# Shifted hidden columns: writing them contiguously from a strided PSUM read, four loads per small weight, and a new order table

## The chip, the cores and the metric

The kernel runs on one core of one Trainium2 chip. The metric is the device time of one execution in microseconds (us); the number given for a kernel is the median of several executions. A profiled execution is one more run, and its span (first to last instruction) is a little shorter than its device time.

## The reference

One sequence of S = 2048 rows with D = 512 columns passes through four residual layers, A, B, A, B, each with a layer norm ahead of it. A is attention with 32 heads of 16 columns over 8 positions at distances 0, 2, ..., 14. B is a mixer:

```
h  = gelu(layernorm(x) @ w1)                      # 2048 x 512
g0 = h[:,   0:128] shifted by +1 row              # rows outside are zero
g1 = h[:, 128:256] shifted by -1 row
g2 = h[:, 256:384] shifted by +2 rows
g3 = h[:, 384:512] shifted by -2 rows
x1 = x + concat(g0, g1, g2, g3) @ w2
out = x1 + gelu(layernorm(x1) @ w3) @ w4          # w3: 512 x 1792, w4: 1792 x 512
```

The change sits in the shift of the four column groups of h.

## The kernel before

**Units of work.** The 2048 rows are four blocks of 512, and there are two passes over them (layers A and B, then A and B again), so the work comes as eight blocks n = 0 to 7. A block has four row tiles of 128 rows. Row tiles are interleaved: tile i of a block holds the row pairs 2i, 2i+1, then the pair eight rows further on, and so on (`rows`). For a block the phases are `p1_stream` (q, k, v through TensorE), `p2_unit` (attention, nearly all on VectorE, four units to a block), `p3` (output projection with wo, a layer norm, the product with w1, gelu, and the shifted h), `p4` (product with w2, the second layer norm) and `p5` (w3, gelu, w4, for fourteen slices of 128 hidden columns).

**Precision.** All products from block 1 on are done in float16 with each operand split into a high and a low half (three matmuls for a product, `HLS`). So h is stored twice: half 0 is gelu(...) scaled and rounded to float16, half 1 is the remainder. In block 0 the `p5` products are plain float32 (`plain_chunk`).

**How h is made.** In `p3`, for each group g of 128 hidden columns, twelve matmuls fill one PSUM buffer of kind "mm" with h transposed: 128 hidden columns on the partitions, 512 rows of the block along the free axis. ScalarE applies gelu in place, then copies the PSUM tile to half 0 of h (`to(0)` from `of()`), and VectorE writes half 1 with one `scalar_tensor_tensor` (`to(1)`). For g = 0 and 1 the shift is by one row, which crosses from a row tile to its neighbour, so the destination `to` walks h in float16 with steps of 127 elements between neighbours, while PSUM is read in order. For g = 2 and 3 the shift by two rows moves whole pairs, and both sides are contiguous. Rows that cross the wrapped end of a tile are then put in their place by copies within h: `move` to the cells "L" (g = 0, 2) and "R" (g = 1, 3), of 126 or 252 elements for each partition, and to "Le" and "Re" (one or two columns for each half, from or to the block next door). GpSimd (POOL) or VectorE does them. A tile of h has HW = 640 columns for each half and group; `p4` reads the 128 columns for row tile i at `RD[g] + P * i`.

**Order.** Nothing is scheduled at run time. Every piece of work is an operation with one or more alternatives (the same work on ScalarE, VectorE or POOL). The table `ORDER` lists all 3135 operations; an entry k stands for operation k // 4 done by its alternative k % 4. Each engine, and the SyncE queue (SP) that issues the DMAs, works through its own part of that list strictly in order. The table `SLOTS` says which physical buffer each logical buffer gets: there are four PSUM buffers "mm" and four "acc", five "f32" row tiles, two of "h", and so on. An operation that writes a buffer waits until all users of what was in it are done. So a PSUM buffer with a group of h in it is free only after gelu, half 0 and half 1.

**Small weights.** `small_weight` loads wo, w1 or w2 (512 x 512 float32, 1 MB) with one DMA into a buffer of kind "nT" or "h", takes its sum of squares (`square`), a matmul with ones (`power_of`), and splits it into halves. The buffer "h" that w1 goes into holds a part of wqkv at first, and is free when the first block's q, k, v products are done.

Every instruction is recorded by one helper, so all lines in the profile read L281.

Of the kernel before, what the change touches and what calls it, by code (L numbers as in the profile page):

```python
# [8 lines left out]
F32 = mybir.dt.float32  # L9
BF16 = mybir.dt.bfloat16  # L10
I32 = mybir.dt.int32
AF = mybir.ActivationFunctionType
# [5 lines left out]
P = 128  # L18
S = 2048
D = 512  # L20
# [12 lines left out]
HW = 640  # L33
# [234 lines left out]
def tile_mixer(ctx, tc, x_d, wqkv_d, wo_d, w1_d, w2_d, w3_d, w4_d, out_d):  # L268
# [575 lines left out]
    def p2_unit(n, qt):  # L844
# [76 lines left out]
        else:  # L921
            turn_split(ko, o, oT, [0], lambda: hl(0), lambda: hl(1), [o], scale=c_o)
        return oT

    RD = (0, P, 0, P)
    hs, n1_st, mixed = {}, {}, {}

    def late(h, g, first, pairs):
# [308 lines left out]
```

## Time and profile before

| | |
|---|---|
| median of 3 runs | 1246.36 us (1244.55 to 1248.82) |
| profiled execution | 1247.58 us |
| its span | 1245.8 us |
| mean granted TensorE clock | 0.977 |
| TensorE (PE) busy | 1166.2 us, 94%, 5324 matmul instructions |
| VectorE (DVE) busy | 955.5 us, 77% |
| ScalarE (ACT) busy | 586.0 us, 47% |
| GpSimd (POOL) busy | 441.7 us, 35% |

In the rows of the profile, an entry such as `h<-mm,c_h` names what is written and what is read; `mm` is a PSUM buffer, `w_hl` the halves of w1 or w2, `nT` a transposed normalized block. `[3.24 <-DVE h]` behind a TensorE row says that TensorE sat idle for 3.24 us ahead of it and what the wait ended with. A matmul's listed time is its latency; the distance between the starts of two groups of twelve is what they cost.

### The profile page before, as it was taken

Reading aid. Unit: us, or ns where it says so; the run is one execution under the profiler, and the core shown is the slowest. Engines: PE = TensorE matmul, PEld = TensorE weight load, DVE = VectorE, ACT = ScalarE, POOL = GpSimd, SP = SyncE. Lnnn points to the kernel's source line nnn. Section 1 sums busy time; section 2 is a strip of 40 time slices with the busy share of each in tenths; the row PEclk is TensorE's granted clock in tenths of the full one; section 3 lists DMA queues with packets and bytes.
Section 4 is the critical chain, followed back from the end, with each engine's and each line's share of the span. In section 5 each row is a group of like instructions: output and inputs, shape, how many; then the busy total and the mean of one; then the engine's idle time right before and its main releaser. Section 6 shows DMA issues by size and latency. Waiting matters only on the chain. (4 is left out here: it accounts for less than half of the span.)

```text
span 1245.8 us, 15079 instructions
## 1 busy us (share of the span) xinstructions
PE 1166.2 (94%) x5324; PEld 551.6 (44%) x5324; DVE 955.5 (77%) x990; ACT 586.0 (47%) x984; POOL 441.7 (35%) x502
## 2 busy tenths in 40 slices
PE   9769999899698999999999998999899999889997
PEld 7434444454243444444444443444344344434553
DVE  6889899998888899549998998699858997223311
ACT  5465454333856645435362356354455454433421
POOL 3110443204556354422672445344254141313000
PEclk9979999899999999999999998999999999999999
DMA  6765683464789546665479563976369366304321
GB/s 222 255 193 145 189 270 104 127 196 154 211 209 304 159 114 159 158 200 188 127 189 259 186 179 81 243 217 168 81 174 261 110 136 186 93 28 117 102 92 53
DMA packets 240388, 206.79 MB, mean 166 GB/s; under 512 B 107132, under 2 KB 167796, under 8 KB 240312
## 3 DMA queue, kind: packets, MB, share of 16 engines
q1 hardware_dynamic: 238088, 204.04, 57.4%
q10 hardware_dynamic: 2224, 1.79, 0.4%
q8 instruction: 42, 0.69, 0.2%
q14 instruction: 34, 0.28, 0.1%
HBM read 141.03 MB, written 39.47 MB: 145 GB/s over the span
## 5 line engine op out<-in xcount | busy, mean ns | idle before, releaser
L281 PE MATMUL mm<-nT,w 128*128 128x512 f16 (+1 forms) x1288 | 306.8, 392 | 9.3 <-DMA w<-w 4.2
L281 PE MATMUL acc<-w,g 128*128 128x512 f16 (+1 forms) x1260 | 306.6, 394 | 0.0
L281 PE MATMUL mm<-wq_hl,xt 128*128 128x512 f16 x1008 | 229.4, 384 | 8.5 <-DMA xt<-g 3.8
L281 ACT ACTIVATE mm<-mm,s_w 128x512 f32<-128x512 f32 (+1 forms) x144 | 92.5, 643 | 225.4 <-PE mm L281 225.2
L281 POOL TENSOR_TENSOR g<-f,g 128x512 f16<-128x512 f32 x80 | 126.7, 1589 | 197.4 <-ACT g L281 98.1
L281 PEld LDWEIGHTS <-w 128*128 128x128 f16 x1344 | 125.3, 98 | 151.2 <-issue 7.8
L281 PEld LDWEIGHTS <-g 128*128 128x128 f16 x1176 | 114.6, 98 | 137.0
L281 PEld LDWEIGHTS <-xt 128*128 128x128 f16 x1008 | 99.3, 99 | 130.2 <-issue 12.2
L281 DVE TENSOR_TENSOR prod<-kv,L 128x4096 f32<-128x4096 f32 x32 | 141.2, 4413 | 0.2
L281 DVE TENSOR_REDUCE L<-prod 128x256 f32<-128x4096 f32 x32 | 141.1, 4410 | 0.1
L281 DVE TENSOR_TENSOR prod<-kv,q 128x4096 f32<-128x4096 f32 x29 | 129.8, 4475 | 9.3 <-DMA kv<-kvq_d 8.8
L281 DVE TENSOR_TENSOR prod<-prod 128x2048 f32<-128x2048 f32 x64 | 117.0, 1829 | 0.2
L281 DVE SCALAR_TENSOR_TENSOR g<-mm,c_g,g 128x512 f16<-128x512 f32 x56 | 41.8, 747 | 97.0 <-ACT g L281 94.1
L281 PE MATMUL mm<-nT,w_hl 128*128 128x512 f16 x384 | 93.5, 397 | 18.5 <-DVE h L281 10.8
L281 PE MATMUL mm<-w_hl,h 128*128 128x512 f16 x384 | 90.9, 393 | 9.1 <-DVE h L281 8.2
L281 PE MATMUL mm<-wo_hl,oT 128*128 128x512 f16 x384 | 86.3, 380 | 0.0
L281 POOL TENSOR_SCALAR b<-b 128x1 f32<-128x1 f32 (+1 forms) x48 | 28.4, 591 | 155.4 <-ACT junk L281 153.4
L281 POOL COPY h<-h 128x126 f16<-128x126 f16 (+3 forms) x40 | 37.2, 949 | 128.0 <-DVE h L281 102.2
L281 DVE SCALAR_TENSOR_TENSOR h<-mm,c_h,h 128x512 f16<-128x512 f32 x32 | 51.0, 1625 | 36.8 <-ACT h L281 36.5
L281 PEld LDWEIGHTS <-w_hl 128*128 128x128 f16 x384 | 38.7, 101 | 70.5 <-issue 29.1
L281 ACT ACTIVATE g<-mm,c_g 128x512 f16<-128x512 f32 x98 | 66.7, 685 | 2.4 <-ACT mm L281 0.4
L281 PEld LDWEIGHTS <-h 128*128 128x128 f16 x384 | 38.5, 101 | 58.4 <-issue 16.9
(183 smaller groups left out, 1361.8 us busy)
## 6 DMA issues: line engine op xcount, KB each, us to landing
w<-w SPq DMA_DIRECT2D x196, 256.0 KB, 2.9
kv<-kvq_d SPq DMA_DIRECT2D x62, 768.0 KB, 5.8
kvq_d<-ev SPq DMA_DIRECT2D x84, 256.0 KB, 3.0
w<-in_B_w_dram SPq DMA_DIRECT2D x56, 256.0 KB, 3.5
w<-g SPq DMA_DIRECT2D x28, 256.0 KB, 4.0
q<-kvq_d SPq DMA_DIRECT2D x28, 256.0 KB, 3.6
w<-in_A_x_dram SPq DMA_DIRECT2D x16, 256.0 KB, 4.2
x<-in_A_x_dram SPq DMA_DIRECT2D x16, 256.0 KB, 4.3
```

Of the source, the lines that this page charges most:

```text
L281: i = f(*a, **k).ins
```

## The change

1. `HW` falls from 640 to 576. The h tile is no longer the rows in one run with spare columns at an end, but three runs: for g = 0 and 2 the first three shifted tiles in columns 0 to 383 and the wrapped one at 384; for g = 1 and 3 the wrapped one at `TAIL` = 388. `COL` replaces `RD`.
2. Both halves are written contiguously. The shift of g = 0 and 1 is now in the pattern by which PSUM is read (steps of two elements and of 127). Each copy becomes two instructions, one of 384 and one of 128 elements for each partition, for all four groups, on ScalarE (`early`) and on VectorE (`later`).
3. The wrapped tile lands in place, so the copies to "L" and "R" are gone (32 operations). The edge copies "Le" and "Re" and the clears stay, and are contiguous.
4. `small_weight` issues four DMAs of 256 KB, one for each 128 rows, where there was one of 1 MB. That is nine DMAs more.
5. "f32" has six buffers instead of five.
6. `ORDER` and `SLOTS` are new tables, for 3112 operations. Of the 518 TensorE operations, 437 stand at another place in TensorE's own sequence. The alternatives differ too: VectorE has 836 operations instead of 871, ScalarE 817 before and 836 now, POOL 285 before and 269 now.

```diff
-HW = 640
+HW = 576
+TAIL = 388
...
-        "f32": places("f32", 5, [P, D], F32),
+        "f32": places("f32", 6, [P, D], F32),
...
-        dma(key - 3.0, lambda: v().rearrange("p (c f) -> p c f", c=NC),
-            lambda: wd.rearrange("(c p) f -> p c f", p=P), [], [(st, c) for c in range(NC)], begun)
+        for c in range(NC):
+            dma(key - 3.0, lambda c=c: v()[:, D * c:D * c + D], lambda c=c: wd[P * c:P * c + P], [], [(st, c)], begun)
...
-    RD = (0, P, 0, P)
+    COL = ((3 * P, 0, P, 2 * P), (0, P, 2 * P, TAIL))
...
-            def to(a, g=g):
+            def parts_of(a, g=g, ps=ps):
+
                 v = blocks(h.t, HW)[:, a, g]
+                e = 2 if g > 1 else 1
+                c0 = 3 * P + e if g % 2 == 0 else TAIL - e
+                t0, s0 = (3 * P, 0) if g % 2 == 0 else (0, P)
                 if g < 2:
-                    return at(v[:, 1:], [list(v.ap[0]), [P, NT], [2, 64], [P - 1, 2]])
-                return v[:, P:] if g == 2 else v[:, :D]
-
-            def of(ps=ps, g=g):
-                return ps.t.rearrange("p (i k r) -> p i k r", i=NT, r=2) if g < 2 else ps.t
+                    src = [at(ps.t[:, 1:], [list(ps.t.ap[0]), [P, 3], [2, 64], [P - 1, 2]]),
+                           at(ps.t, [list(ps.t.ap[0]), [2, 64], [3 * P + 1, 2]])]
+                else:
+                    src = [ps.t[:, s0:s0 + 3 * P], ps.t[:, t0:t0 + P]]
+                return zip((v[:, :3 * P], v[:, c0:c0 + P]), src)
+
+            def early(parts_of=parts_of):
+                for o, i_ in parts_of(0):
+                    A.activation(o, i_, AF.Copy, scale=c_h.t)
+
+            def later(parts_of=parts_of):
+                for (o, i_), (hi, _) in zip(parts_of(1), parts_of(0)):
+                    V.scalar_tensor_tensor(o, i_, c_h.t, hi, ALU.mult, ALU.subtract)
...
-            act(key, lambda of=of, to=to: A.activation(to(0), of(), AF.Copy, scale=c_h.t),
-                [ps, c_h], [(h, (g, 0))])
-            dve(key, lambda of=of, to=to: V.scalar_tensor_tensor(
-                to(1), of(), c_h.t, to(0), ALU.mult, ALU.subtract), [ps, (h, (g, 0)), c_h], [(h, (g, 1))])
+            act(key, early, [ps, c_h], [(h, (g, 0))])
+            dve(key, later, [ps, (h, (g, 0)), c_h], [(h, (g, 1))])
...
-                move((h, ("L", g)), lambda g=g, n_=n_: late(h, g, 2, n_), lambda g=g, n_=n_: late(h, g, D, n_), own)
...
-                move((h, ("R", g)), lambda g=g, n_=n_, f0=f0: late(h, g, D + f0, n_),
-                     lambda g=g, n_=n_, f0=f0: late(h, g, 2 + f0, n_), own)
...
-                    c0 = RD[g] + P * i
+                    c0 = COL[g % 2][i]
```

More of the change, by code (lines that the diff above doesn't have):

```diff
@@ L43 @@
 ORDER = [int(k) for k in """
[139 rows of a table removed]
[138 rows of a table added]
 """.split()]
 SLOTS = """
-0021310010001002102011010310012012310100123001678111334533206732113103000140150144222673010564461510564407231065301645
-2142560273112645720311061273101307010000212200100010120001013211010000230100100100032111000102001000031021100120100003
-0101001101330020011010211001000001111011010010311030000311031000103001012000000511100111016201200000143100011101400011
-0010101320113010230310021121201111200010033000011101610100110010212200100040436810303012122033012022330113302332634012
@@ L189 @@
-3136541607122013321563041631510045327003470642354304720500003333310300132131200023510234223513620134350120657210042332
-0037612422106115502412116011243713412136200312001003312031312313120310111120002010101111100010003301200000020101011000
-4214630441320212334200203140100451230211472351302111120023436467151024347210513127243521461144025372063522211041011201
-0021100031011211011410212111201010052001000001401020111003101100000143827022001301432100110113400214140003214024230216
-0325410370121026641527024241245020341141026640347205040415104102121202211010212102100105203120121011000010020001012310
@@ L194 @@
-1010001220220011004064151321020102111012010123130142335420223233102131346247005152001622103262621143247605153036126430
-0224200140101202041400312021130012120200002111201000160001001100011020100015301100110032238723302462113040022000200420
-4100232040247031250224623320621004572026235402127233030222334153043623473645164022612060000122110122451023231251241031
-2210362041722303344636572140214672222123372024126572521721071426283514002351302451011122040322212330112411002121272310
-1315234534221201230630223506232633225622227424326105334131030306331232035305037
+0021310010001002202011010300011021121320123112126220234511165731103110111040510164056273301425324722141610563265024153
@@ new lines @@
+2226156270320233130522534663723462011100112200020000120011011210011100131102001011101130011033021301021120300020111002
+0110002201330120022013210101120031111310010000110021101200110112000111002001200411110122001210101220003002001200300110
+0113101110310110331002020111313010101220031002002200221020022000000101220063672000011122031122103000121221311020126012
+7526643323110611171025361413211406220720502645121611341523101123023212010200240123420160211431702132121402452201160330
+2117205642600522210034331570431616300537113002110000012030202210031115112020012012100331010012012000201220142101001100
@@ new lines @@
+4167280441300123234210203206100142045411060103210201045341300476220235453366404421213430417254003156217025024052121314
+0610211141531003100221102011100110002020011100601110012006112100110163401321401212252462002003320425622521004300120133
+2304624500557311262650312611053413151404505752632001562303112202020311202020502000000001002131111002101110020112010210
+2011101100010011000372562501023112204002122316110010332325403213120414072216533030364225350102101176060325541205616323
+1171255021101012020330013001300112111221101101100110011120011100200210011015312000110142410805403232323010112100430534
@@ L199 @@
+4302252164266210352653102272540410652121722341542503073046414153647431541203523724411111231431010140100113422465205235
+4301202206116752103220012435423261601715462103722671000734522307014610411452422051123101231412332260246432511263242103
+3224123600110122125205116121132113217126234322131005035603133216110715024603001
 """
@@ L923, in p2_unit @@
         return oT
-    RD = (0, P, 0, P)
+    COL = ((3 * P, 0, P, 2 * P), (0, P, 2 * P, TAIL))
     hs, n1_st, mixed = {}, {}, {}
-    def late(h, g, first, pairs):
-        v = h.t.rearrange("p (a g f) -> p a g f", a=2, g=NC)[:, :, g]
-        k = 2 if g < 2 else 1
-        return v[:, :, first:first + k * (pairs - 1) + 1:k] if k > 1 else v[:, :, first:first + pairs]
     def p3(n):
@@ L1013, in clear, with edge @@
                 gp(key, lambda: G.memset(dst(), 0.0), own, [cell], also=[(DVE, lambda: V.memset(dst(), 0.0), None)])
-            n_, e_ = (63, 1) if g < 2 else (126, 2)
+            def edge(t, c0, g=g):
+                e = 2 if g > 1 else 1
+                return t.t.rearrange("p (a g f) -> p a g f", a=2, g=NC)[:, :, g, c0:c0 + e]
+            e = 2 if g > 1 else 1
             if g % 2 == 0:
-                move((h, ("L", g)), lambda g=g, n_=n_: late(h, g, 2, n_), lambda g=g, n_=n_: late(h, g, D, n_), own)
-                edge = lambda g=g, e_=e_: late(h, g, 0, e_)
+                to = lambda edge=edge: edge(h, 3 * P)
                 if hprev is None:
-                    clear((h, ("Le", g)), edge)
+                    clear((h, ("Le", g)), to)
                 else:
-                    move((h, ("Le", g)), edge, lambda g=g, e_=e_: late(hprev, g, HW - 2, e_),
-                         own + [(hprev, [(g, 0), (g, 1)])])
-            else:
-                f0 = 1 if g == 1 else 0
-                move((h, ("R", g)), lambda g=g, n_=n_, f0=f0: late(h, g, D + f0, n_),
-                     lambda g=g, n_=n_, f0=f0: late(h, g, 2 + f0, n_), own)
+                    move((h, ("Le", g)), to, lambda edge=edge: edge(hprev, 4 * P), own + [(hprev, [(g, 0), (g, 1)])])
+            else:
                 if hprev is not None:
-                    move((hprev, ("Re", g)), lambda g=g, e_=e_, f0=f0: late(hprev, g, HW - 2 + f0, e_),
-                         lambda g=g, e_=e_, f0=f0: late(h, g, f0, e_), own)
+                    move((hprev, ("Re", g)), lambda edge=edge, e=e: edge(hprev, TAIL + P - e),
+                         lambda edge=edge, e=e: edge(h, TAIL - e), own + [(hprev, [(g, 0), (g, 1)])])
                 if b == NB - 1:
-                    clear((h, ("Re", g)), lambda g=g, e_=e_, f0=f0: late(h, g, HW - 2 + f0, e_))
+                    clear((h, ("Re", g)), lambda edge=edge, e=e: edge(h, TAIL + P - e))
     def h_cells(i):
@@ L1035, in h_cells @@
         if i == 0:
-            c += [(s, g) for s in ("L", "Le") for g in (0, 2)]
+            c += [("Le", g) for g in (0, 2)]
         if i == NT - 1:
-            c += [(s, g) for s in ("R", "Re") for g in (1, 3)]
+            c += [("Re", g) for g in (1, 3)]
         return c
```

277 rows, old and new, of the table ORDER are left out of this document.

## The prediction

> **What bounds the kernel now.** The first page and a table of windows come first, since they say which engine sets the pace and where it does not.
>
> ```profile
> span 1245.8 us, 15079 instructions
> PE 1166.2 (94%) x5324; PEld 551.6 (44%) x5324; DVE 955.5 (77%) x990; ACT 586.0 (47%) x984; POOL 441.7 (35%) x502
> ...
> 300.00:400.00 100.00, 85.24 (x351) 38.06 (x350) 85.51 (x124) 61.94 (x118) 52.51 (x67) 0.95 0.81 229
> 600.00:700.00 100.00, 100.00 (x465) 45.22 (x463) 91.44 (x85) 47.11 (x80) 61.70 (x49) 1.00 0.73 207
> 1000.00:1100.00 100.00, 93.18 (x424) 41.59 (x423) 60.43 (x65) 51.16 (x75) 31.86 (x41) 0.98 0.51 131
> ```
>
> The columns of a window are its length, the busy time (and instructions) of PE, weight load, DVE, ACT and POOL, the granted clock, the DMA share and GB/s. TensorE is the bound: from 600 to 700 us it never pauses, and 465 matmuls fit there. From 1000 to 1100 it fits 424 of the same kind, with DVE at 60%, so what is missing there is not another engine's throughput but waits. The view of waits, for TensorE alone, names them (us in total, times, longest):
>
> ```profile
> PE mm L281 <- DVE h L281: 20.3, 9, 4.1
> PE mm L281 <- ACT w_hl L281: 13.1, 2, 11.5
> ...
> PE mm L281 <- DVE ev L281: 0.3, 1, 0.3
> ```
>
> Its twenty rows, of which the first two and the last are shown, add up to 72.6 us. The first is h, the tile that the change touches, the second a small weight. The timeline shows how h makes TensorE wait; the last block is the clearest place (rows of PE, ACT and DVE; start, length, then idle time before it in brackets):
>
> ```profile
> 1084.06 2.75 PE L281 MATMUL mm<-nT,w 128*128 128x512 f16 x12
> 1090.06 4.13 PE L281 MATMUL mm<-nT,w_hl 128*128 128x512 f16 x12 [3.24 <-DVE h L281]
> 1100.02 4.27 PE L281 MATMUL mm<-nT,w_hl 128*128 128x512 f16 x12 [3.24 <-DVE h L281]
> 1104.12 2.75 PE L281 MATMUL acc<-w,g 128*128 128x512 f16 x12
> 1106.71 2.75 PE L281 MATMUL mm<-nT,w_hl 128*128 128x512 f16 x12
> ...
> 1084.26 0.66 ACT L281 ACTIVATE mm<-mm,s_w 128x512 f32<-128x512 f32 x1 [0.57 <-PE mm L281]
> 1084.96 2.53 ACT L281 ACTIVATE h<-mm,c_h 128x512 f16<-128x512 f32 x1
> 1105.02 0.69 ACT L281 ACTIVATE h<-mm,c_h 128x512 f16<-128x512 f32 x1
> ...
> 1087.52 2.48 DVE L281 SCALAR_TENSOR_TENSOR h<-mm,c_h,h 128x512 f16<-128x512 f32 x1 [8.86 <-ACT h L281]
> 902.91 0.75 DVE L281 SCALAR_TENSOR_TENSOR h<-mm,c_h,h 128x512 f16<-128x512 f32 x1 [1.47 <-ACT h L281]
> ```
>
> Group 0 of h is done on TensorE at 1084.1; gelu takes 0.66, the strided ACT copy 2.53, the strided DVE remainder 2.48, and at 1090.06, 5.8 us after the gelu began, TensorE gets the PSUM buffer back. It had one group of twelve matmuls (2.59 us from start to start, as 1104.12 to 1106.71) to do meanwhile: 5.8 - 2.6 = 3.2, the wait shown. The same copies for groups 2 and 3 take 0.69 and 0.75: same shape, contiguous. The stride costs 1.8 us on each engine.
>
> A wait costs more than itself. The twelve matmuls behind it take 4.13 or 4.27 us instead of 2.75, and the granted clock of that stretch is low:
>
> ```profile
> 763.11 10.64 PE L281 MATMUL mm<-w_hl,h 128*128 128x512 f16 x36 [4.13 <-DVE h L281]
> 892.21 4.07 PE L281 MATMUL mm<-nT,w_hl 128*128 128x512 f16 x12 [3.25 <-DVE h L281]
> 993.79 4.44 PE L281 MATMUL mm<-w_hl,h 128*128 128x512 f16 x12 [2.58 <-DVE h L281]
> ...
> 1084.00:1106.00 22.00, 15.52 (x59) 6.26 (x57) 6.37 (x8) 10.66 (x11) 2.46 (x4) 0.84 0.08 25
> ```
>
> 36 matmuls at full rate are 2.75 + 2 x 2.59 = 7.93, so the row at 763 loses 2.7, and the others 1.3, 1.7, 1.4 and 1.5: 8.6 us behind five waits. Late h costs 20.3 + 8.6 = 28.9 us.
>
> **The copies of h (parts 1 and 2).**
>
> ```profile
> L281 ACT ACTIVATE h<-mm,c_h 128x512 f16<-128x512 f32 x32 | 51.7, 1614 | 14.1 <-POOL h L281 12.6 <-DVE h L281 0.7
> L281 ACT ACTIVATE g<-mm,c_g 128x512 f16<-128x512 f32 x98 | 66.7, 685 | 2.4 <-ACT mm L281 0.4
> L281 ACT ACTIVATE oT<-mm,c_g 128x128 f16<-128x128 f32 x14 | 5.1, 367 | 0.3
> L281 DVE SCALAR_TENSOR_TENSOR g<-mm,c_g,g 128x512 f16<-128x512 f32 x56 | 41.8, 747 | 97.0 <-ACT g L281 94.1 <-issue 2.6
> L281 DVE SCALAR_TENSOR_TENSOR oT<-mm,c_g,oT 128x128 f16<-128x128 f32 x14 | 4.9, 347 | 5.4 <-ACT oT L281 5.4
> L281 DVE COPY h<-h 128x252 f16<-128x252 f16 x5 | 1.1, 221 | 0.0
> L281 DVE COPY h<-h 128x126 f16<-128x126 f16 x3 | 0.7, 238 | 0.1
> L281 DVE COPY h<-h 128x4 f16<-128x4 f16 x4 | 0.6, 150 | 0.1
> ```
>
> Between 128 and 512 elements ACT adds 318 ns for 384 and DVE 400, so a 384 copy is some 0.58 on ACT and 0.61 on DVE, and the new pair 0.95 and 0.96 if reading PSUM at a stride is free: the lower bound, and the price for groups 2 and 3, which lose 0.26 and 0.21 each. No row shows a strided PSUM read. The upper bound is that hops cost as much in reading as they did in writing: 2.53 + 0.26 = 2.79 and 2.48 + 0.21 = 2.69. The nearest rows are the last three: 252 contiguous elements cost 71 ns over four, 126 at a step of two 88, which is 0.28 and 0.70 ns an element, 0.42 more for the stride, or 0.21 us for 512. I take that: about 1.16 and 1.17 for groups 0 and 1. [...]
>
> The chain from gelu to a free buffer becomes 0.66 + 1.16 + 1.17 + 0.1 = 3.1 for groups 0 and 1 (before 5.8), and 0.66 + 0.95 + 0.96 + 0.1 = 2.7 for 2 and 3 (before 2.2). Busy time changes by 16 x 1.37 - 16 x 0.26 = 18 us less on ACT and 16 x 1.31 - 16 x 0.21 = 18 less on DVE; on TensorE only the waits count.
>
> How much of the waiting remains is read from the new table: how much TensorE work, at 2.59 for a group, stands between a group of h and the next use of its PSUM buffer, and between the last group and the first product of p4. For groups 0 and 1 of blocks 0 to 7 that is now 8.4/3.7, 5.3/10.6, 7.8/7.8, 7.8/7.8, 5.2/7.8, 36/7.8, 2.6/5.2 and 7.8/23.3; against 3.1 only block 6 falls short, by 0.5. For groups 2 and 3 and p4 the short places are block 1, where group 3's buffer is wanted at once (2.7), and blocks 4 and 6 with 2.6 against 2.7. Before, the last block had 2.6 for each group, hence its two waits. Sum: 2.7 + 0.5 + 0.4 = 3.6; with 2 us for places where DVE is inside a 4.4 us instruction when h comes, 5.6 of 20.3 remain, and one slow start of 1.6 of 8.6. Gain: 14.7 + 7.0 = 21.7 us.
>
> **The wrapped copies (part 3).**
>
> ```profile
> L281 POOL COPY h<-h 128x126 f16<-128x126 f16 x13 | 15.5, 1190 | 56.3 <-DVE h L281 38.1 <-DVE mx L281 15.2 <-ACT h L281 3.1
> L281 POOL COPY h<-h 128x252 f16<-128x252 f16 x11 | 10.8, 983 | 27.0 <-DVE h L281 27.0
> ```
>
> These 24 and the eight on DVE go: 26.3 us of POOL, 1.8 of DVE. POOL at 35% was not the bound, but p4's row tiles 0 and 3 had to wait for the copies, and ACT sat 12.6 us behind POOL on h (the row above). If they hid entirely the gain is nothing. I put 1 us on it.
>
> **Four loads for a small weight (part 4).**
>
> ```profile
> 59.21 0.38 SPq L281 DMA_DIRECT2D h<-in_B_w_dram  x1
> 67.79 0.77 POOL L281 TENSOR_SCALAR f<-w,a,a 128x512 f32<-128x512 f32 x1
> 68.15 1.91 ACT L281 ACTIVATE w_hl<-h 128x2048 bf16<-128x2048 f32 x1 [2.46 <-DMA h<-in_B_w_dram]
> 70.21 0.59 PE L281 MATMUL mm<-ss_w,ones 128*128 128x1 f32 x2 [11.51 <-ACT w_hl L281]
> ```
>
> w1's megabyte is issued at 59.21 and lands near 68.1; its sum of squares is the next thing in TensorE's order, hence 11.5 us of idle. The square still needs all four parts. Nine more issues of about 0.4 us lie on SP, 3.4 us, at 42 to 60 us, ahead of the x rows; POOL's and ACT's queues are not passed. What helps is the order: two transposes, two subtractions and two groups of matmuls now stand ahead of that sum. They need f, ready at 68.6, so the wait ends 1.6 us sooner at best; bounds are 11 us gained, were the rows of x to come early, and 3.4 lost. I take 2 gained.
>
> **Sixth f32 buffer and new order (parts 5 and 6).** 35 fewer operations on DVE, 27 of them moved (some 0.5 to 0.7 us each), ease an engine that is 91% busy from 600 to 700 us; 1 us for that. Waits other than h are 72.6 - 20.3 = 52.3 us, and the new order reshuffles all of them: zero on average, 12 us either way as the bound of my ignorance, about a quarter of them.
>
> **Sum.** 21.7 + 1 + 2 + 1 = 25.7 less than the profiled 1247.6 (span 1245.8 and 1.8 around it), 1221.9. The median of the runs is 1.2 lower, so 1221.
>
> **The rivals.** *The new order gives it back.* h is no longer late, but other waits grow from 52.3 by 10 to 20 us, around 300 to 400 us above all, where PE is 85% busy and DVE the same. For it: five sixths of TensorE's sequence moved. Against: DVE has less to do. 1238.
>
> *Reading at a stride is as dear as writing was.* Then the chain of groups 0 and 1 is 0.66 + 2.79 + 2.69 + 0.1 = 6.2, and by the distances above TensorE lacks 2.5 (block 0), 0.9 (1), 1.0 (4), 3.6 and 1.0 (6), with block 1's group 3 and the 2 us for DVE 14 us in all; seven slow starts at 1.6 add 11. 25 against 28.9 is a gain of 4; with 1 for the copies and 2 for the load, none for DVE, the time is 1247.6 - 7 - 1.2 = 1239. For it: no row excludes it. [...] Against: the stride rows of DVE above.
>
> *Slower: the third block's attention comes late.* The last of its four output transposes is issued at 366.81; the 24 DMAs of this form land after 3.5 us in the median; TensorE starts on it at 372.42, so some 2 us are to spare.
>
> ```profile
> 366.81 1.25 SPq L281 DMA_TRANSPOSE oT<-g  x1
> oT<-g SPq DMA_TRANSPOSE x24, 3.5
> 372.42 2.75 PE L281 MATMUL mm<-wo_hl,oT 128*128 128x512 f16 x12
> ...
> 0.00:372.00 372.00, 330.04 (x1389) 171.84 (x1390) 328.32 (x347) 184.73 (x357) 119.16 (x147) 0.96 0.62 190
> ```
>
> Summed by row means, the new order puts 3 us more DVE work ahead of that point and 5 us more TensorE work. Each us that DVE idles longer up to there ends on the total one for one. It was idle for 372 - 328 = 44 us there; the rival decides from some 30 us more, when the 25 are gone and 4 besides. About 1256.
>
> **How the numbers follow.** A difference of 0.3% (3.7 us) is about what a measurement of this kernel can tell. Chances: the forecast 0.58 (1209 to 1233), better still, with startup gains, 0.05, the order giving it back 0.18 (1233 to 1251), the dear read 0.09 (1233 to 1251), the late attention 0.10 (from 1246). Under 1242.6 lie 0.58 + 0.05 + 0.14 of the 0.18 + 0.05 of the 0.09 = 0.82. Within 0.3% lie 0.03 + 0.03 + 0.02 of the last = 0.08. Slower: 0.01 + 0.01 + 0.08 = 0.10. The range leaves out the best 0.05 and the slower cases: 1207 to 1244.
>
> **What would show it.** Right: TensorE's waits on DVE h fall from 20.3 to some 6 us; the last block's two waits of 3.24 are gone; the ACT copies of h are 384 and 128 wide at about 0.6 to 0.8 and 0.37; POOL has only narrow copies of h. Wrong: 384-wide copies of 2 us or more (the dear read), TensorE's other waits well above 52 us (the order), or among them a wait of the third block's wo product on its transposes (the late attention). The start is right if the 11.5 us idle near 60 us has shrunk a little.

## The result, and the profile after

| | before | after |
|---|---|---|
| median | 1247.59 us (1244.55 to 1251.42) | 1210.30 us (1208.85 to 1212.04) |
| profiled execution, its span | 1247.58, 1245.8 us | 1210.33, 1208.4 us |
| granted TensorE clock | 0.977 | 0.987 |
| waits of TensorE, all rows | 72.6 us | 45.2 us |

The ratio is 0.970, 95% interval 0.967 to 0.973: 37 us less, where 25.7 had been forecast. The head of the page and two rows of the table of windows:

```profile
span 1208.4 us, 15153 instructions
...
PE 1158.0 (96%) x5324; PEld 550.2 (46%) x5324; DVE 921.4 (76%) x988; ACT 573.3 (47%) x1036; POOL 430.9 (36%) x486
...
300.00:400.00 100.00, 90.32 (x388) 40.22 (x387) 87.62 (x122) 67.80 (x131) 53.91 (x58) 0.93 0.86 252
...
1000.00:1100.00 100.00, 98.28 (x455) 44.45 (x456) 44.57 (x73) 39.64 (x70) 30.14 (x49) 1.00 0.44 115
```

The same 5324 matmuls take 8.2 us less busy time (1166.2 before), which fits fewer slow starts behind waits; TensorE's idle time falls from 1245.8 - 1166.2 = 79.6 to 50.4 us. Together that is the 37.4 us of span. From 1000 to 1100 us 455 instructions fit where there were 424. TensorE's waits after, the largest and the one on h, of twenty rows:

```profile
PE mm L281 <- DMA xt<-g: 7.8, 2, 5.8
PE mm L281 <- DVE mx L281: 5.2, 1, 5.2
PE mm L281 <- ACT ev L281: 5.2, 5, 2.7
PE mm L281 <- POOL f L281: 5.1, 2, 3.5
...
PE mm L281 <- DVE h L281: 0.6, 1, 0.6
```

By name, the 20.3 us on DVE h are 0.6, and the 13.1 on ACT w_hl are gone from the list; what is left is spread out, and one of its rows hides a wait for h (in the part on the prediction). The last block's groups of h, by the timeline of TensorE, ScalarE and VectorE:

```profile
1053.26 2.75 PE L281 MATMUL mm<-nT,w_hl 128*128 128x512 f16 x12
1055.85 2.75 PE L281 MATMUL mm<-nT,w 128*128 128x512 f16 x12
1058.44 2.75 PE L281 MATMUL acc<-w,g 128*128 128x512 f16 x12
...
1056.05 0.66 ACT L281 ACTIVATE mm<-mm,s_w 128x512 f32<-128x512 f32 x1 [0.63 <-PE mm L281]
1056.74 0.84 ACT L281 ACTIVATE h<-mm,c_h 128x384 f16<-128x384 f32 x2
...
1057.62 0.88 DVE L281 SCALAR_TENSOR_TENSOR h<-mm,c_h,h 128x384 f16<-128x384 f32 x2 [4.53 <-ACT h L281]
```

From gelu (1056.05) to the free PSUM buffer (1057.62 + 0.88) it is 2.45 us, before 5.8, and less than one group of twelve matmuls (2.59). No spacing in these rows of TensorE is over 2.59. The copies with their shapes kept apart:

```profile
L281 ACT ACTIVATE h<-mm,c_h 128x384 f16<-128x384 f32 x32 | 18.6, 581 | 0.7
L281 ACT ACTIVATE h<-mm,c_h 128x128 f16<-128x128 f32 x32 | 11.8, 367 | 0.0
L281 DVE SCALAR_TENSOR_TENSOR h<-mm,c_h,h 128x384 f16<-128x384 f32 x32 | 19.6, 611 | 22.1 <-ACT h L281 22.0
L281 DVE SCALAR_TENSOR_TENSOR h<-mm,c_h,h 128x128 f16<-128x128 f32 x32 | 10.9, 342 | 0.0
```

Half of each row's 32 read PSUM at a stride, and the means are those forecast for contiguous reading (0.58, 0.61, 0.37, 0.35). The two halves don't stand apart either: all 32 copies of 384 lie between 561 and 607 ns on ScalarE and between 602 and 618 on VectorE. No cost of the stride shows on the reading side.

### The profile page after: what moved, and what is told of

Read it like the earlier page. It is cut to its first block, busy times and chain, and to the rows that moved or that the text cites. A ratio compares the mean times of both kernels' runs of the same rounds, so it can differ in the third digit from the quotient of the medians.

```text
span 1208.4 us, 15153 instructions
## 1 busy us (share of the span) xinstructions
PE 1158.0 (96%) x5324; PEld 550.2 (46%) x5324; DVE 921.4 (76%) x988; ACT 573.3 (47%) x1036; POOL 430.9 (36%) x486
## 4 chain that ended last, share of the span: by engine, by line
PE 69%; DMA 10%; DVE 9%; issue 5%; ACT 4%; POOL 2%; SPq 1%; DVEq 0%; ACTq 0%; POOLq 0%
PE mm L281 50%; PE acc L281 19%; DVE prod L281 3%; DMA kv<-kvq_d 2%; DMA kvq_d<-ev 2%; DVE L L281 2%; DMA nT<-g 1%; DMA w<-in_A_x_dram 1%; DVE g L281 1%; SPq L281 1%; ACT junk L281 1%; DMA xt<-g 1%; DVE x L281 1%; POOL b L281 1%; POOL x L281 1%
## 5 line engine op out<-in xcount | busy, mean ns | idle before, releaser
L281 PE MATMUL mm<-nT,w_hl 128*128 128x512 f16 x384 | 87.6, 379 | 1.7 <-DMA nT<-g 1.5
L281 PE MATMUL mm<-w_hl,h 128*128 128x512 f16 x384 | 86.5, 379 | 0.7 <-DVE h L281 0.6
L281 PEld LDWEIGHTS <-oT 128*128 128x128 f16 x426 | 42.4, 100 | 54.6 <-issue 7.1
L281 PEld LDWEIGHTS <-h 128*128 128x128 f16 x384 | 37.4, 98 | 46.3 <-DVE h L281 1.1
```

What stands on the lines that cost most here:

```text
L281: i = f(*a, **k).ins
```

## The experiments

Each ratio is to the kernel before, run on the same chip.

**1. The copies alone.** The new p3 and its h tile, the rest as before: the old table without the 32 wrapped copies, five f32 buffers, one load for each weight.

```diff
 # from the changed kernel
-ORDER, SLOTS: the new tables
+ORDER, SLOTS: the old tables, less the operations "L" and "R"
-        "f32": places("f32", 6, [P, D], F32),
+        "f32": places("f32", 5, [P, D], F32),
-        for c in range(NC): dma(... 256 KB ...)
+        dma(... 1 MB ...)
```

> The order table and the buffers of the kernel before (the 32 wrapped copies taken out of the table), one load for each small weight, with the new contiguous copies of h. Theory 1 (the shorter copies themselves end the waits): TensorE's waits on h fall from 20.3 us to about 5, with fewer slow starts behind them, and the time is about 1225 us (1220 to 1231). Theory 2 (the new order, which leaves more TensorE work between a group of h and the next use of its buffer, does nearly all of it): 1240 us or more, within 0.5% of the kernel before.

Measured: 1214.54 us (1213.54 to 1217.12), ratio 0.972 (0.970 to 0.974); the whole change had 0.970 (0.967 to 0.973). Theory 1 holds, and more is gained than it said (1220 to 1231). The intervals overlap: by the medians the order, the loads and the sixth buffer add 4 us, by the ratios 2, and that can't be told from nothing. Two of this kernel's waits, and the last block's rows:

```profile
PE mm L281 <- ACT w_hl L281: 12.6, 2, 11.3
...
PE mm L281 <- DVE h L281: 2.7, 1, 2.7
```

```profile
1060.38 2.75 PE L281 MATMUL mm<-nT,w_hl 128*128 128x512 f16 x12
1062.97 2.75 PE L281 MATMUL mm<-nT,w 128*128 128x512 f16 x12
1065.67 2.76 PE L281 MATMUL mm<-nT,w_hl 128*128 128x512 f16 x12
1068.28 2.75 PE L281 MATMUL mm<-nT,w 128*128 128x512 f16 x12
...
1081.58 4.71 PE L281 MATMUL mm<-w_hl,h 128*128 128x512 f16 x21
```

In the old order, with one group between a group of h and the next use of its buffer, the 3.24 us wait has become 0.11 (1062.97 to 1065.67 is 2.70 instead of 2.59). The 11.3 us wait for the weight near 70 us stands, and the whole change, which does not have it, is no more than those 2 to 4 us faster.

**2. Is it the distance between the writes?** The order of the whole change, PSUM read in order, and h written with 32 bytes between neighbours for groups 0 and 1.

```diff
-                    src = [at(ps.t[:, 1:], [list(ps.t.ap[0]), [P, 3], [2, 64], [P - 1, 2]]),
-                           at(ps.t, [list(ps.t.ap[0]), [2, 64], [3 * P + 1, 2]])]
+                    src = [ps.t[:, s0:s0 + 3 * P], ps.t[:, t0:t0 + P]]
+                    dst = [at(v, [w0, [1, 16], [16, 24]]), at(v[:, c0:], [w0, [1, 16], [16, 8]])]
```

> The changed kernel with its order, but for groups 0 and 1 PSUM is read contiguously and h is written with 32 bytes between neighbours (the columns of h land in another order than the reference's). Theory 1: the write is what was dear, so each 384 copy takes about 1.9 us instead of 0.58 (ACT) and 0.61 (DVE) and the chain of groups 0 and 1 grows from 2.6 to about 6 us; by the distances in the table TensorE waits 10 to 14 us more with slow starts behind, 1222 to 1238 us. Theory 2: the new order has room for the long copies, within 5 us of the changed kernel's 1210.

Measured: 1232.16 us (1228.23 to 1234.35), ratio 0.985 (0.983 to 0.988). Copies (by shape) and wait:

```profile
L281 ACT ACTIVATE h<-mm,c_h 128x384 f16<-128x384 f32 x32 | 39.9, 1246 | 0.7
L281 DVE SCALAR_TENSOR_TENSOR h<-mm,c_h,h 128x384 f16<-128x384 f32 x32 | 39.5, 1233 | 28.3 <-ACT h L281 28.3
```

```profile
PE mm L281 <- DVE h L281: 15.4, 9, 4.4
```

Half of the 32 are contiguous at 581, so the far ones take 2 x 1246 - 581 = 1911 ns on ScalarE, 3.5 ns more for each of 384 elements; on VectorE it is 2 x 1233 - 611 = 1855. ScalarE's copy is the clean case, since only its write is far. VectorE's instruction also reads half 0 of h at the same far step (as it did in the kernel before), so what its write alone costs isn't shown. Nine waits on h are back, and 22 of the 37 us are lost although the table is the new one.

**3. Or the half-filled words?** A step of two elements (4 bytes) in reading and in writing; every destination word is still written in two goes.

```diff
+                    src = [at(ps.t[:, 1:], [q0, [P - 1, 2], [2, 192]]), at(ps.t, [q0, [3 * P + 1, 2], [2, 64]])]
+                    dst = [at(v, [w0, [1, 2], [2, 192]]), at(v[:, c0:], [w0, [1, 2], [2, 64]])]
```

> The changed kernel, but groups 0 and 1 are copied with a step of two on both sides: neighbours are 4 bytes apart in h, so each write fills half of a 4-byte word, and the result is the same. If half-filled words are what makes a strided float16 write dear: copies of 384 take about 1.9 us, time as for the far writes. If it is the distance between neighbours: 0.6 us, and 1210 within 3 us.

Measured: 1210.33 us (1208.10 to 1219.44), ratio 0.971 (0.966 to 0.975), the time of the changed kernel.

```profile
L281 ACT ACTIVATE h<-mm,c_h 128x384 f16<-128x384 f32 x32 | 20.4, 636 | 0.7
L281 DVE SCALAR_TENSOR_TENSOR h<-mm,c_h,h 128x384 f16<-128x384 f32 x32 | 20.1, 627 | 22.7 <-ACT h L281 22.6
```

By the same sum a copy at a step of two is 691 ns on ScalarE, 0.29 ns more for each element. It is the far step that is dear (1911 ns at 32 bytes in 2, and 2.53 us for 512 elements at 254 in the kernel before), not the half-filled word.

**4. One load for each weight.** The whole change with its fourth part undone.

```diff
-        for c in range(NC): dma(... 256 KB ...)
+        dma(... 1 MB ...)
```

> The changed kernel with one DMA of 1 MB for each small weight, in the place of the first of the four. Theory 1: the sum of squares needs the whole weight, so the split changes nothing: within 4 us of 1210. Rival: the split lets the loads land sooner and is part of why the 11.5 us wait at the start is gone: 1216 us or more.

Measured: 1212.64 us (1210.86 to 1217.37), ratio 0.971 (0.968 to 0.973). No difference that can be measured.

**5. The wrapped copies put back.** Kernel 1 with the 32 operations at their old places, copying columns onto themselves.

```diff
+            move((h, ("LR"[g % 2], g)), again, again, own)    # again: 126 or 252 columns, in place
```

> The old order with the new copies, and the 32 wrapped copies back in their places, of the same width and on the same engines (24 on POOL, 8 on VectorE), now copying a part of h onto itself; p4 waits for them as before. Theory 1 (part 3 is worth 1 to 3 us, the copies of h nearly all): 1215 to 1219 us. Rival (the copies on POOL, up to 4.5 us long beside VectorE, held up p4 and ScalarE): 1222 us or more.

Measured: 1215.73 us (1213.15 to 1216.88), ratio 0.973 (0.971 to 0.975), against 0.972 (0.970 to 0.974) without them. Part 3 is worth some 1 us by this, and the intervals allow nothing as well as 4 us.

**6. Another buffer for a wait at the start.** In the changed kernel TensorE waits 5.2 us near 60 us for a PSUM buffer that VectorE holds. One entry of `SLOTS` gives that product another buffer.

> The changed kernel with one digit of the buffer table changed: the last product of the first block's q, k, v goes to another PSUM buffer, so that it no longer waits 5.2 us (near 60 us) for VectorE to read the sum of squares of w2. The wait for DVE mx of 5.2 us should go. Theory 1: the next thing that TensorE needs, the normalized rows f, is ready at 67 us either way, so the time stays within 2 us of 1210. Rival: the loads behind it (w1, k and v of the first block) start 5 us sooner and the time falls by 4 us or more.

Measured: 1210.53 us (1209.27 to 1216.39), ratio 0.970 (0.967 to 0.973), the time of the changed kernel. TensorE's timeline in the changed kernel, then in this one, there with VectorE's:

```profile
60.82 4.87 PE L281 MATMUL mm<-h,g 128*128 128x384 f32 x8 [5.20 <-DVE mx L281]
67.29 1.09 PE L281 MATMUL mm<-ident,f 128*128 128x128 f32 x8 [1.60 <-POOL f L281]
```

```profile
61.27 4.35 PE L281 MATMUL mm<-h,g 128*128 128x384 f32 x8 [5.52 <-DVE x L281]
67.99 1.97 PE L281 MATMUL mm<-ident,f 128*128 128x128 f32 x8 [2.37 <-POOL f L281]
...
56.46 4.42 DVE L281 TENSOR_TENSOR prod<-kv,q 128x4096 f32<-128x4096 f32 x1 [2.59 <-DMA w<-g]
60.93 0.28 DVE L281 TENSOR_SCALAR x<-mm 128x128 f32<-128x128 f32 x1
```

The wait is as long under another name, so this run doesn't test what its removal is worth. The other buffer is one that VectorE empties too (the copy x at 60.93), and both reads stand in VectorE's queue behind the same attention instruction of 4.42 us. That the wait matters little is argued, not shown: what TensorE needs next, the tile f, comes at 67 to 68 us either way.

**7. The short copies, with scratch work behind them.** Kernel 1, and behind the copies of groups 0 and 1 five scratch instructions of 256 elements on both engines. They write tiles of their own.

```diff
             def early(parts_of=parts_of, g=g):
...
+                if g < 2:
+                    for _ in range(5): A.activation(pad_a, pad_a, AF.Copy)
             def later(parts_of=parts_of, g=g):
...
+                if g < 2:
+                    for _ in range(5): V.scalar_tensor_tensor(pad_v, pad_v, c_h.t, pad_v, ALU.mult, ALU.subtract)
```

> The old order with the new copies (1214.5 us), and behind the two copies of each group 0 and 1, on ScalarE and on VectorE, five scratch instructions of 256 elements from SBUF (about 1.7 to 2 us each engine and group), which nobody waits for: the engines are as busy with h as before the change, but the PSUM buffer is free as early as after it. Theory 1 (what counted was how long a group of h holds its PSUM buffer and its chain): at most 8 us over 1214.5. Rival (what counted was the time of ScalarE and VectorE): back to 1235 us or more.

Measured: 1249.60 us (1243.59 to 1255.04), ratio 1.000 (0.998 to 1.002). The scratch stands behind the copy, so it doesn't lengthen the hold of that copy's own buffer; yet the whole gain is gone, as the rival had it. Some 4 of these us were lost at the start, where filling the scratch tile stood first in ScalarE's queue (block 0's products with wq begin at 79.87 us, in the next kernel at 75.74). The scratch is also longer than meant, here from the next kernel:

```profile
L281 DVE SCALAR_TENSOR_TENSOR padv<-padv,c_h 128x256 f32<-128x256 f32 x80 | 40.8, 510 | 2.3
L281 ACT ACTIVATE pada<-pada 128x256 f32<-128x256 f32 x80 | 33.3, 417 | 2.0
```

Five of them are 2.55 us on VectorE and 2.08 on ScalarE, where the change took 1.6 and 1.7 off such a copy (2.48 to 0.88, 2.53 to 0.84). So that just the whole gain is lost is in part chance. The next four runs fill the tile elsewhere and split the scratch.

**8 to 11. Which engine, and where.** As 7 with both; VectorE's alone; ScalarE's alone; and both engines' scratch moved out of p3, VectorE's behind the residual sums at the end of p5, ScalarE's behind high halves of g.

```diff
 # the last of the four
                 V.scalar_tensor_tensor(x.t, acc[k].t, ..., x.t, ALU.mult, ALU.add, **more)
+                for _ in range((3, 3, 2, 2, 0)[k] if K > 3 else (4, 3, 3)[k]):
+                    V.scalar_tensor_tensor(pad_v, pad_v, c_h.t, pad_v, ALU.mult, ALU.subtract)
```

> The same scratch instructions on both engines behind the copies of groups 0 and 1, with scratch buffers that hold nothing up at the start. Theory 3: 1240 to 1248 us, as in the padded kernel before, less some 5 us that its start lost. Theory 1 (only how long the PSUM buffer is held): at most 1222.

> Scratch instructions behind the copies of groups 0 and 1 on VectorE alone. Theory 3: VectorE is the fuller engine and its long attention instructions stand in the same queue, so most of the loss is here, 1228 to 1240 us. Rival (ScalarE's queue, where the next gelu stands, is the one that matters): under 1222.

> Scratch instructions behind the copies of groups 0 and 1 on ScalarE alone. Theory 3: 1218 to 1228 us, less than on VectorE. Rival: 1230 or more.

> The old order with the new copies (1214.5 us), and the scratch instructions (80 on VectorE, 70 on ScalarE, some 27 and 29 us in all) moved out of p3: on VectorE behind the residual sums at the end of p5, on ScalarE singly behind the high halves of g in p5. Theory 3 (what counts is time on ScalarE and VectorE inside the h stage, in the copies or right behind them, where the next group and p4 queue): 1215 to 1226 us. Rival (engine time wherever it lies, VectorE being near its limit): 1238 us or more.

| scratch | median us | ratio |
|---|---|---|
| none (kernel 1) | 1214.54 | 0.972 (0.970 to 0.974) |
| both, in p3 | 1247.35 | 0.999 (0.997 to 1.001) |
| VectorE, in p3 | 1247.89 | 0.999 (0.997 to 1.002) |
| ScalarE, in p3 | 1219.67 | 0.978 (0.974 to 0.981) |
| both, in p5 | 1244.07 | 0.997 (0.995 to 0.999) |

VectorE's 80 instructions add 40 us to its busy time (929.2 to 969.0) and cost 33 by the medians, more than theory 3 had (1228 to 1240); ScalarE's add 31 (562.8 to 593.6) and cost 5, hardly clear of the spread. (Kernel 1 ran on another chip, where the kernel before took 1249.16 instead of 1248.60.) And both cost about as much in p5, against theory 3 (1215 to 1226). One reading is that VectorE's own time is the price, wherever it is spent. That is a theory with a plain test.

**12. Taking time off VectorE where no copy of h is.** The kernel before, with the 32 sums in the attention shortened.

```diff
-            Lv(), pv4().rearrange("p t j (h d) -> p t j h d", d=DH), AX.X, ALU.add), [pr], [L])
+            Lv(), pv4().rearrange("p t j (h d) -> p t j h d", d=DH)[:, :, :, :, :14], AX.X, ALU.add), [pr], [L])
```

> The kernel before, with its copies of h, its table and its loads untouched; only the sums over the 16 products of a head in the attention (32 reductions, DVE L<-prod, 4410 ns each before, 141.1 us together) take 14 of the 16, so part of the computation is left out. That takes about 2/16 of 141.1 = 17.6 us off VectorE (down to 15 if the shorter rows cost something of their own), all of it in the attention ahead of p3, none in the copies of h. Theory A (VectorE's own time is what counts, wherever it is spent; the scratch work gave about one us for each): 17.6 us less, 1247 to about 1229, ratio about 0.986, between 0.983 and 0.990; the waits named after h shrink although no copy of h is shorter, since the queue reaches them earlier. Theory B (the gain of the change is that the copies of h themselves are short, the holds of four buffers and the chain of g0 and g1): their waits stay near 20 us, the attention's units end somewhat earlier but p3 starts when TensorE gets there; 1243 to 1247, ratio 0.997 to 1.000. In between (1235 to 1241): both, in shares that this run gives.

Measured: 1246.10 us (1242.29 to 1250.02), ratio 0.998 (0.997 to 1.000). The head of the page and the group that was cut:

```profile
span 1241.0 us, 15079 instructions
...
PE 1163.0 (94%) x5324; PEld 551.5 (44%) x5324; DVE 935.9 (75%) x990; ACT 585.5 (47%) x984; POOL 438.3 (35%) x502
...
L281 DVE TENSOR_REDUCE L<-prod 128x256 f32<-128x3584 f32 x32 | 124.1, 3878 | 0.1
```

```profile
PE mm L281 <- DVE h L281: 19.6, 10, 4.1
```

VectorE is relieved of 955.5 - 935.9 = 19.6 us, about as much as the change itself saves on the copies of h (51.0 to 30.5), and the time stays: theory A falls, B holds, for time taken from the attention. The waits on h are as before.

**All of it in one table.** The kernels with the old table share TensorE's sequence, so their timelines can be cut at the same two places in each of the eight blocks: the h stage is from the start of the first product with w1 to the start of the first with w2 (the last block of kernel 1, above: 1060.38 to 1081.58; of the kernel before: 1081.47 to 1111.89). Sums over the blocks, from the profiled executions:

| old table, with | h stages us | rest of the span us |
|---|---|---|
| long copies (before) | 207.5 | 1038.3 |
| long copies, shorter sums | 205.2 | 1035.8 |
| short copies (kernel 1) | 179.0 | 1036.3 |
| and VectorE scratch in p3 | 204.3 | 1038.6 |
| and ScalarE scratch in p3 | 181.7 | 1036.0 |
| and both scratches in p3 (8) | 204.8 | 1043.8 |
| and both, filled late (7) | 203.6 | 1048.6 |
| and scratch in p5 | 179.9 | 1068.7 |

The rest is the same within 3 us in the first five kernels, 5.5 us above the first in 8 (whose profiled execution is 3 us above its median) and higher in the last two. The copies take 28.5 us off the h stages and 2.0 off all else; VectorE's scratch puts 25.3 back into the stages, ScalarE's 2.7. The scratch in p5 leaves the h stages alone and costs 32.4 elsewhere. With 12 beside it I read this as another sensitive place, and not as a sign that VectorE's total counts. (Its profiled execution is 6 us above its median, so up to 6 of the 32 may be that, and which engine's scratch costs how much of it wasn't separated.) Its last block shows one such wait (VectorE, then TensorE):

```profile
1154.17 1.52 DVE L281 SCALAR_TENSOR_TENSOR padv<-padv,c_h 128x256 f32<-128x256 f32 x3
1155.60 0.35 DVE L281 SCALAR_TENSOR_TENSOR oT<-mm,c_g,oT 128x128 f16<-128x128 f32 x1
...
1156.01 0.39 PE L281 MATMUL mm<-w,oT 128*128 128x512 f16 x1 [2.93 <-DVE oT L281]
1156.94 4.39 PE L281 MATMUL mm<-nT,w 128*128 128x512 f16 x12
```

VectorE is a third busy there (32.46 of the 100 us from 1100 on), and still TensorE waits 2.93 us for a copy that is queued behind scratch, and starts slowly after it (the twelve matmuls at 1156.94 are listed with 4.39 us, elsewhere 2.75). In p3 the same happens to h, here in block 4 of the kernel with VectorE's scratch:

```profile
760.57 4.42 DVE L281 TENSOR_TENSOR prod<-kv,L 128x4096 f32<-128x4096 f32 x1
764.90 0.87 DVE L281 SCALAR_TENSOR_TENSOR h<-mm,c_h,h 128x384 f16<-128x384 f32 x2
765.69 3.33 DVE L281 SCALAR_TENSOR_TENSOR padv<-padv,c_h 128x256 f32<-128x256 f32 x5
768.94 1.66 DVE L281 SCALAR_TENSOR_TENSOR h<-mm,c_h,h 128x384 f16<-128x384 f32 x4
...
770.74 2.72 PE L281 MATMUL mm<-w_hl,h 128*128 128x512 f16 x6 [8.62 <-DVE h L281]
```

VectorE's queue holds the copies of h one behind the other, with attention work between them (here 4.42 us). What stands between two copies here delays those behind it: the four at 768.94 start when 3.33 us of scratch are done, and with their end at 770.60 the wait of 8.62 us ends and TensorE goes on, at 770.74. ScalarE has only short instructions between its copies here, of 0.81 us at most. This accounts for 7 as well: scratch behind group 0 is ahead of group 1.

## Why the prediction was right, and where its sizes were off

**The bound, held.** It said that waits, not another engine's throughput, are what TensorE lacks. Experiments 8 to 11 put that in doubt, and 12 speaks for it: with 19.6 us less of VectorE's time in the attention the ratio is 0.998 (0.997 to 1.000). That is one place; in 11 VectorE's time counts where TensorE waits on its queue.

**The price of h, right, its rows incomplete.** Late h was put at 20.3 of waits and 8.6 of slow starts. The row DVE mx, 5.6 us, belongs to it too: each of its three waits ends right behind a copy of h of 2.49 us on VectorE. One of them in the kernel before (VectorE, TensorE), and VectorE at the same place in kernel 1:

```profile
188.43 2.49 DVE L281 SCALAR_TENSOR_TENSOR h<-mm,c_h,h 128x512 f16<-128x512 f32 x1 [1.70 <-ACT h L281]
190.53 0.41 DVE L281 RECIPROCAL mx<-mx 128x32 f32<-128x32 f32 x1
...
190.97 3.25 PE L281 MATMUL mm<-wq_hl,xt 128*128 128x512 f16 x9 [2.02 <-DVE mx L281]
```

```profile
186.28 0.86 DVE L281 SCALAR_TENSOR_TENSOR h<-mm,c_h,h 128x384 f16<-128x384 f32 x2
187.06 0.33 DVE L281 RECIPROCAL mx<-mx 128x32 f32<-128x32 f32 x1
```

By the table `SLOTS` the product at 190.97 takes the PSUM buffer of a group of h. The h copy ends at 190.92, 0.05 ahead of TensorE's start; the small reciprocal behind it ended last (190.94) and gave the wait its name. In kernel 1 no wait on mx is left, and its other waits are 46.4 - 2.7 = 43.7 instead of 52.3, of which 5.6 are this row.

**The copies' gain, 21.7 forecast, mis-sized.** In kernel 1 the h stages are 28.5 us shorter and the span 30.5 (34.6 by the medians of 1). Of the 30.5, waits on h are 17.6 (20.3 to 2.7; 14.7 forecast), the row mx 5.6 and other waits 3.0; TensorE's busy time falls by 4.1, where 7.0 of slow starts were forecast. So in the old order the surplus is the overlooked row and a smaller residue; the slow starts were worth less than said. For the whole change the span falls by 37.4: waits on h by name give 19.7 (14.7 forecast), all other rows 7.7 (52.3 to 44.6; 4 forecast), busy time 8.2 (7.0) and gaps too short for the view 1.8.

The chain was priced too long. The strided read was put at 0.42 ns an element from copies in SBUF, and shows no cost (all copies of 384 lie between 561 and 607 ns on ScalarE and between 602 and 618 on VectorE), and two copies issued in a row take less than the sum of their means (581 + 367 and 611 + 342 ns): a pair takes 0.84 on ScalarE and 0.88 on VectorE, below the lower bound of 0.95 and 0.96. So the chain from gelu to a free buffer is 2.45 us where 3.1 was taken, and with 2.45 against 2.59 for one group the places forecast as short by a few tenths (0.9 of the residue of 5.6) are no longer short.

The largest place of the residue, block 1 with 2.7 us, is still there, under another name. TensorE (two rows) and VectorE in the changed kernel:

```profile
312.30 5.34 PE L281 MATMUL mm<-nT,w_hl 128*128 128x512 f16 x24
323.46 4.87 PE L281 MATMUL mm<-wq_hl,xt 128*128 128x512 f16 x12 [5.82 <-DMA xt<-g]
...
320.68 0.86 DVE L281 SCALAR_TENSOR_TENSOR h<-mm,c_h,h 128x384 f16<-128x384 f32 x2
```

TensorE is idle from 317.64. The next product takes the buffer of group 3, whose copies on VectorE end at 321.54, 3.9 us later; the transposed rows xt come last, at 323.46, and give the wait its name. If the DMA had come earlier, the wait would still have been some 3.9. With the 0.6 by name that is 4.5 us of residue, near the 5.6 forecast, and the fall to 0.6 is in part a change of name.

**The dear read, out.** The trace has a mean of 611 ns on VectorE for 384 elements with half of the copies strided, and 581 on ScalarE, where 0.61 and 0.58 us had been worked out for contiguous ones; the rival needed copies of 2 us or more, and the longest take 618 and 607 ns.

**The small terms, about right in sum.** One us for the wrapped copies (5: some 1 us), two for the loads and the order at the start, one for VectorE's relief, and zero for the table: together 4, against 2 to 4 measured between kernel 1 and the whole change, and 1 for the wrapped copies, none of them clear of the noise. The loads themselves give nothing that shows (4), and no run shows the one us for VectorE's relief (12 found none for time taken from the attention). That the sum agrees is in part luck. None of the rivals came: the order gave nothing back, and no wait of the third block's wo product on its transposes is in the list.

**The start, half right.** The 11.5 us wait is gone by name. Waits of 5.20, 1.60 and shorter ones stand in its place, and block 0's products with wq begin at 69.69 instead of 73.78; what removing the largest of them would give isn't shown, since experiment 6 left it in place.

## What to carry to other kernels

Price a copy by the chain that holds a buffer, and compare it with the work that the waiting engine has meanwhile: in the old order the wait of 3.24 us fell to 0.11 once the chain was shorter than that work. Adding time to an engine does not show that its total counts (here 40 us more on VectorE cost 33, and 19.6 us less elsewhere on it gave no gain that shows); cut time elsewhere on the same engine as well, and split the span at fixed places to see where each difference sits. Read a wait's name together with the instruction ahead of the named one in that engine's queue: a short instruction (0.41 us) behind a long copy (2.49 us) gave its name to the copy's delay, and where two things were awaited, ready at 321.54 and 323.46 us, the name showed only the later one.

## What the runs showed of the hardware

Writing float16 far apart is dear on ScalarE: for 384 elements 1911 ns at 32 bytes, 691 at 4 bytes, 581 contiguous, and for 512 elements 2.53 us at 254 bytes in the kernel before, 0.69 contiguous. VectorE's instruction is as dear (1855 ns at 32 bytes, 611 contiguous, 2.48 us at 254), but there half 0 is read at the same step, and no run has the write alone. Reading float32 from PSUM in a pattern with strides of two and of 127 elements showed no cost on either engine: of the 32 copies of 384 elements half read so, and all took 561 to 607 ns on ScalarE and 602 to 618 on VectorE. What in the write path sets the price was not tried; the runs only place it between a step of 4 and one of 32 bytes.
